# Retention chunks and a Mish layer on one core: outer products as half-array matmuls behind the present terms, states kept as 64x64 blocks, and two products in exchanged order

## The chip, the core and the metric

The kernel runs on one core of one Trainium2 chip. The metric is device time in microseconds (us), the median of some runs. The kernel before took 203.49 us (three runs, 203.35 to 203.62). The engines are TensorE (PE: matmuls, and PEld for its weight loads), VectorE (DVE), ScalarE (ACT), GpSimd (POOL) and SyncE (SP, which here only issues DMAs).

## The reference

Two stages. The first is a linear recurrence for 4 batches and 8 heads over 768 steps with head size 64, the second a two-layer net on its output.

```
gamma = 1.0 - 2.0 ** (-5.0 - np.arange(H))
for t in range(S):
    state = gamma * state + k[t] (outer) v[t]        # 64 x 64 per batch and head
    y[t] = scale * (q[t] @ state)
x = y as (B * S, H * D)                              # 3072 x 512
h = x @ w_in                                         # 512 x 2048
g = h * tanh(log(1 + exp(h)))                        # Mish
return g @ w_out                                     # 2048 x 512
```

## The kernel before

**Chunks.** The recurrence is done in chunks of 128 steps; a batch has 6 of them (`NCH`), so there are 24 chunks, numbered g through all batches. For a chunk the kernel makes the scores k·q (`scores`, L387), masks them to the lower triangle on DVE (`mask`, L397), and adds two terms into one PSUM tile `y_ps`: the past term, state times q (`past`, L430), and the present term, masked scores times v (`present`, L437). The decay factors are folded into the casts of q and v to 16 bits, which POOL makes (`cast_q`, L328, and `cast_v`, L343); k comes through POOL's DMA queue as 16 bits (`bring_k`, L333); the transposed q and k come by DMA on SP's queue (`turn_by_dma`, L356).

**States.** The state after chunk g is (u + state before) times gamma^128, where u is the outer product k·v over the 128 steps of the chunk (`outer`, L404). Two heads share one 128x128 matmul: the four pairs of heads give a tile of 128 x 512, in which the two diagonal 64x64 blocks of each pair are the wanted states, and the other two blocks are mixed products of two different heads. The factor tile `gcm` holds gamma^128 in the diagonal blocks and zero elsewhere, so that the multiplication also clears the mixed blocks. `state_sum` (L412) adds u and the state before on DVE, `state_decay` (L421) multiplies by `gcm`, on POOL in the later blocks. At the first chunk of a batch there is no state before, and `state_sum` multiplies at once (L416). The last chunk of a batch needs no state. `past` uses the 128x128 tile of a pair of heads as weights.

**Blocks.** The second stage takes the chunks in blocks: block 0 has 4 chunks, blocks 1 to 10 have 2 each (256 rows). Block 0 and the weights fill the first 51.5 us. In block 1 only the first layer is done by the seven-product method, in blocks 2 to 10 both layers are:

- `g1_seven` (L617) makes h for half of its tiles with seven products of quarter size instead of eight (`mm`, L636: eight matmuls of 128x128 weights by 128 columns each, L639), from sums and differences of weights (`wsum`) and of x (`tsums`, made by `x_sums`, L608), and the other half with four plain products (`plain`, L659: eight matmuls by 256 columns, L663). Three PSUM tiles pb, px and pe are used again within a block: ACT copies an intermediate value out (`snap`, L643), and the next product then adds onto the tile in place. DVE adds a copy to a tile (`plus`, L654) for c11, c22 and c12, and ACT applies Mish to g.
- `seven` (L714) does the same for the second layer (`mm`, L733, 256 columns), with sums of g (`gsum`) that DVE makes, and ACT's copies `snap` (L738) m1, u2, m5.

The order of everything is written by hand: the pool of schedules is off (`manual_schedule`), so each engine carries out its instructions in the order of the Python text. `steps_of(blk)` (L953) names what is put between the products of a block: after the second product ("p2"), behind some later ones ("p6", "p7", "p4", "h2", "end"), and in `seven` ("m2", "m7", "m3"). While block `blk` is computed, `nb = blk + 1` gets ready: its first chunk is a - 2 and its second a - 1, where a = first[blk] + 4. In "p2" stand the outer products of both chunks of nb (`outer_next`, L933), the sum and the decay of the first; in "p7" the sum of the second, in "m2" its decay; in "h2" the scores of both; in "m7" the past and present terms (`y_two`, L479), whose result ACT copies to 16 bits (L489); in "m3" the sums of x for the next block. Block 1 has a plan of its own (`plan_of`, L985).

The order of the products in `g1_seven`, with what each of them waits for: a(0,0) into px, which ACT copies as m1; a(0,1) into pb (c11 = pb + m1); "p2"; then s(2) added into px (copy u2) and s(1) into pe (copy m5), in this order where nb has two outer products (`sum_first`), else in the other; plain(1,0); s(3) added into px, for which u2 must have been read; c22 = px + m5 on DVE; s(4) added into pe, for which m5 must have been read; c12 = pe + u2; "p7"; plain(3,0); a(1,1) added into px, for which c22 must have been read; plain(1,1); scores ("h2"); plain(3,1).

Two PSUM rings hold all this: `mmps` with 4 tiles for the second stage, `atps` with 2 for scores, u and y.

Of the kernel before, what the change touches and what calls it, by code (L numbers as in the profile page):

```python
# [9 lines left out]
FP16 = mybir.dt.float16  # L10
FP32 = mybir.dt.float32
AF = mybir.ActivationFunctionType
ALU = mybir.AluOpType
# [3 lines left out]
def kernel(  # L17
# [21 lines left out]
    BLOCKS = [4] + [2] * ((NCK - 4) // 2)  # L39
    first = [sum(BLOCKS[:i]) for i in range(len(BLOCKS))]  # L40
# [3 lines left out]
    FPS = NFB // NSL  # L44
# [36 lines left out]
    ident = cpool.tile([P, P], FP16, name="ident")  # L81
    tri = cpool.tile([P, C], FP32, name="tri")
    gcm = cpool.tile([P, HP, P], FP32, name="gcm")
    warm = cpool.tile([P, 1], FP32, name="warm")
    gate_t = cpool.tile([P, 1], FP16, name="gate")
    nc.gpsimd.memset(ident, 0.0)
# [18 lines left out]
    for h in range(H):  # L105
        o = 64 * (h % 2)
        nc.vector.memset(gcm[o:o + 64, h // 2, o:o + 64], float(gamma[h] ** C))

    win_ap = moe_w_in.rearrange("(bp p) f -> p bp f", p=P)
# [3 lines left out]
    raw, k16s, v16s, t16s, kts, amf = {}, {}, {}, {}, {}, {}  # L113
    loaded, cast, qkts, ats, ams, states, us, ys, sus = {}, {}, {}, {}, {}, {}, {}, {}, {}
    xts, gts, wins, wouts, wtmps = {}, {}, {}, {}, {}
    gtiles, tmats, gsums = {}, [], []
# [8 lines left out]

    def room(g):
        loaded[g] = [
            lpool.tile([P, H, D], FP32, name=nm + "f", tag=nm + "f", bufs=4 if nm == "q" else 6)
            if g < BRING or nm != "k" else None for nm in "qkv"]

    def load_one(g, n, queue):
# [89 lines left out]
            eng.tensor_copy(dst, src)  # L221

    def load_two(nm, s, half):
        t = lpool.tile([P, HP, R, D], FP32, name=nm + "f", tag=nm + "f", bufs=6)
# [179 lines left out]
    def outer(g, u_ps):  # L404
        _, k16, v16, _ = cast[g]
        for i in range(HP):
            nc.tensor.matmul(  # L407
                u_ps[:, i], k16[:, 2 * i:2 * i + 2], v16[:, 2 * i:2 * i + 2],
                start=True, stop=True)
        us[g] = u_ps  # L410

    def state_sum(g):  # L412
        u_ps = us.pop(g)
        if g % NCH == 0:
            states[g] = stp.tile([P, HP, P], FP16, name="st")
            nc.vector.tensor_tensor(states[g], u_ps, gcm, op=ALU.mult)  # L416
        else:
            sus[g] = stp.tile([P, HP, P], FP32, name="su")
            nc.vector.tensor_tensor(sus[g], u_ps, states[g - 1], op=ALU.add)  # L419

    def state_decay(g, by):  # L421
        if g in sus:
            states[g] = stp.tile([P, HP, P], FP16, name="st")
            by.tensor_tensor(states[g], sus.pop(g), gcm, op=ALU.mult)  # L424

    def state(g):
        state_sum(g)
        state_decay(g, nc.vector)

    def past(g, y, fresh, pairs=range(HP)):  # L430
        st, qt = states[g - 1], qkts[g][0]
# [15 lines left out]
    def last_of_batch(g):  # L447
        return g % NCH == NCH - 1
# [3 lines left out]
    def scores_one(g):  # L452
        scores(g)
        mask(g)

    def outer_state(g):
        outer(g, atps.tile([P, 2, HP, P], FP32, name="u_ps", tag="at")[:, 0])
        state(g)

    def scores_two(blk):
        a = first[blk]
# [3 lines left out]
        mask(a + 1)  # L467

    def outer_two(blk):
        a = first[blk]  # L470
        u_ps = atps.tile([P, 2, HP, P], FP32, name="u_ps", tag="at")
        for j in range(2):
            if not last_of_batch(a + j):
                outer(a + j, u_ps[:, j])
        for j in range(2):
            if not last_of_batch(a + j):
                state(a + j)

    def y_two(blk):  # L479
        a = first[blk]  # L480
# [136 lines left out]
    def g1_seven(blk, steps, sum_first=False):  # L617
# [9 lines left out]
        def s(i):  # L627
            return lambda f, d: wsums[0][:, i - 1, d, f * P:(f + 1) * P]

        def b(i, j):  # L630
            return lambda d: x_part(blk, i, j)[:, d]

        def t(i):
            return lambda d: tsums[blk][:, i - 1, d]

        def mm(h_ps, w, x, first=False):  # L636
            for f in range(FPS):
                for d in range(n):
                    nc.tensor.matmul(  # L639
                        h_ps[:, f], w(f, d), x(d), start=first and f == 0 and d == 0,  # L640
                        stop=d == n - 1, skip_group_check=True)
# [33 lines left out]
        mm(pb, a(0, 1), b(1, 0), True)  # L675
        c11 = plus(pb, m1)
        step("p2")
        if sum_first:
            mm(px, s(2), t(2))
            u2 = snap(px)  # L680
        mm(pe, s(1), t(1), True)
        m5 = snap(pe)
        if not sum_first:
            mm(px, s(2), t(2))
            u2 = snap(px)
        step("u2")
        mish_of(0, 0, c11)
        step("p6")
        plain(1, 0)
        mm(px, s(3), t(3))  # L690
        c22 = plus(px, m5)
        mm(pe, s(4), b(1, 1))
        c12 = plus(pe, u2)
        mish_of(1, 1, c22)
        mish_of(0, 1, c12)
# [115 lines left out]
    def first_block():  # L811
# [9 lines left out]
        at = at_tile()  # L821
# [62 lines left out]
        for s in range(1, NSL):  # L884
# [12 lines left out]
            24: [(turn, CPB)],  # L897
            25: [(scores_one, CPB)],
            27: [(turn, CPB + 1)],
            28: [(outer_state, CPB), (casts, CPB + 2), (turn_and_load, CPB + 2), (cast_q, CPB + 3)],  # L900
            29: [(scores_one, CPB + 1)],
            31: [(y_two, 1)],
        }
# [26 lines left out]
            turn_by_dma(g)  # L930
            load_to(g + 3)

    def outer_next(blk):  # L933
        a = first[blk]
        u_ps = atps.tile([P, 2, HP, P], FP32, name="u_ps", tag="at")
        for j in range(2):
            if not last_of_batch(a + j):
                outer(a + j, u_ps[:, j])

    def sum_next(blk, j):  # L940
        if not last_of_batch(first[blk] + j):
            state_sum(first[blk] + j)

    def decay_next(blk, j):
        state_decay(first[blk] + j, nc.gpsimd)

    def gate_x(blk):
        gate(tsums[blk][:, 3, 0, :1])
# [24 lines left out]

# [22 lines left out]
    for blk in range(1, len(BLOCKS)):  # L996
        if blk >= SEVEN:
            steps = steps_of(blk)
            g1_seven(blk, steps, blk + 1 < len(BLOCKS) and not last_of_batch(first[blk + 1] + 1))
# [49 lines left out]
```

## Time and profile before

| | |
|---|---|
| median of three runs | 203.49 us |
| the profiled execution | 204.0 us, its span 202.2 us |
| granted TensorE clock in the profile | 0.999 |
| start-up with block 0 | 0 to 51.5 us, PE busy 46.3 |
| block 1 | 51.5 to 67.3 us, PE busy 15.7 |
| blocks 2 to 9 | 67.3 to 186.1 us, PE busy as good as all of it, 14.7 to 15.0 us a block |
| block 10 and the end | 186.1 to 202.2 us, PE busy 12.9 |
| in a block of 14.7 us | DVE busy 11.0, ACT 8.1, POOL 7.8 |

The span is the time from the first to the last instruction; the execution's own time has 1.8 us around it. A row of the groups reads: line, engine, operation, output and inputs, shape, count, busy time in all, mean ns of one, then the idle time of its engine ahead of it and what ended it. A row of the timeline reads: start, length, engine, line, operation, count, and in brackets the idle time before. A matmul's length there includes its way through the array, so that matmuls overlap; what one costs PE is the distance from start to start.

### The profile page before, as it was taken

The page shows a single profiled execution, that of the slowest core. Times are in us where ns is not written, and L with a number is a line of the kernel's source. Part 1 is how long each engine was busy: PE and PEld are TensorE (multiplying, and loading weights), DVE is VectorE, ACT ScalarE, POOL GpSimd, SP SyncE. Part 2 cuts the span into 40 slices and gives each one's busy share as a digit, 9 for nine tenths or more (in the row PEclk, how much of TensorE's full clock was granted, in tenths as well). Part 3 has the DMA queues.
Part 4 walks back from the last instruction along what each step waited for, and adds up shares of the span by engine and source line. Part 5 has one row for each costly group of instructions (what it writes and reads, how often), then busy time and mean ns, then how long its engine had stood idle before and what let it go on. Part 6 is the DMA issues. An engine that isn't in the chain of part 4 may idle for free.

```text
span 202.2 us, 5401 instructions
## 1 busy us (share of the span) xinstructions
PE 193.7 (96%) x2239; PEld 153.0 (76%) x2239; DVE 143.9 (71%) x271; ACT 102.6 (51%) x183; POOL 82.4 (41%) x99
## 2 busy tenths in 40 slices
PE   6897999989999999999999999999999999999993
PEld 2455544445865888988988988988988988989982
DVE  2777693969848687588696696787696696596552
ACT  2363664151960572673573573563663753753840
POOL 4072000617645347646608629626609716200000
PEclk9999999999999999999999999999999999999999
DMA  5999999999899999999991998999992992200202
GB/s 163 303 312 357 386 386 305 270 255 194 150 116 273 253 201 202 144 176 211 188 183 49 151 165 174 167 172 156 209 200 62 186 136 56 105 3 28 80 26 78
DMA packets 95896, 36.55 MB, mean 181 GB/s; under 512 B 82304, under 2 KB 89984, under 8 KB 95872
## 3 DMA queue, kind: packets, MB, share of 16 engines
q1 hardware_dynamic: 75968, 33.30, 73.1%
q0 software_dynamic: 16640, 2.10, 16.4%
q10 hardware_dynamic: 3264, 0.82, 2.3%
q8 instruction: 17, 0.28, 0.6%
q14 instruction: 7, 0.06, 0.1%
HBM read 27.30 MB, written 6.29 MB: 166 GB/s over the span
## 4 chain that ended last, share of the span: by engine, by line
PE 80%; DMA 8%; DVE 6%; ACT 2%; issue 1%; SPq 0%; DVEq 0%
PE o_ps L734 28%; PE h_ps L663 18%; PE h_ps L639 16%; DMA wt<-in_moe_w_out_dram 6%; PE o_ps L526 6%; PE y_ps L443 3%; PE at L393 3%; DMA qfirst<-in_q_dram 2%; PE y_ps L433 2%; PE u_ps L407 2%; DVE tmat L558 1%; PE h_ps L807 1%; ACT xt L489 1%; DVE tmat L560 1%; DVE tmat L559 1%
## 5 line engine op out<-in xcount | busy, mean ns | idle before, releaser
L663 PE MATMUL h_ps<-xt,win 128*128 128x256 f16 x320 | 41.2, 273 | 0.0
L330 POOL TENSOR_TENSOR qk<-qf,qvs 128x512 f16<-128x512 f32 x20 | 24.0, 1199 | 25.5 <-DMA qf<-in_q_dram 25.3
L663 PEld LDWEIGHTS <-win 128*128 128x128 f16 x320 | 29.4, 98 | 3.6
L734 PEld LDWEIGHTS <-gsum 128*128 128x128 f16 x288 | 27.5, 98 | 3.8
L656 DVE TENSOR_TENSOR hsum<-h_ps,hsnap 128x512 f32<-128x512 f32 x30 | 19.8, 688 | 13.7 <-PE h_ps L639 11.4
L399 DVE TENSOR_TENSOR am<-at,tri 128x1024 f16<-128x1024 f32 x20 | 24.2, 1217 | 3.6 <-PE at L393 3.6
L667 ACT ACTIVATE g<-h_ps 128x512 f16<-128x512 f32 x40 | 23.8, 594 | 5.6 <-PE h_ps L663 5.5
L646 ACT COPY hsnap<-h_ps 128x512 f32<-128x512 f32 x30 | 16.6, 588 | 17.6 <-PE h_ps L639 17.6
L734 PE MATMUL o_ps<-tmat,gsum 128*128 128x256 f16 x216 | 25.1, 273 | 0.0
L345 POOL TENSOR_TENSOR v<-vf,qvs 128x512 f16<-128x512 f32 x20 | 21.3, 1063 | 5.2 <-DMA vf<-in_v_dram 5.2
L734 PEld LDWEIGHTS <-g 128*128 128x128 f16 x216 | 21.1, 98 | 2.4
L748 DVE TENSOR_TENSOR osb<-o_ps,snap 128x256 f32<-128x256 f32 x27 | 11.4, 424 | 16.0 <-PE o_ps L734 11.3
L526 PE MATMUL o_ps<-wout,g 128*128 128x512 f16 x96 | 22.7, 379 | 0.0
L489 ACT CAST xt<-y_ps 128x1024 f16<-128x1024 f32 x10 | 10.1, 1012 | 21.9 <-PE y_ps L443 21.9
L650 ACT ACTIVATE g<-hsum 128x512 f16<-128x512 f32 x30 | 18.7, 634 | 4.0 <-DVE hsum L656 4.0
L740 ACT COPY snap<-o_ps 128x256 f32<-128x256 f32 x27 | 10.1, 373 | 19.4 <-PE o_ps L734 19.4
L639 PEld LDWEIGHTS <-wsum 128*128 128x128 f16 x320 | 19.1, 98 | 0.5
L734 PE MATMUL o_ps<-wout,g 128*128 128x256 f16 x144 | 17.2, 273 | 0.0
L354 POOL COPY gate<-gsum 128x1 f16<-128x1 f16 x8 | 1.5, 183 | 37.9 <-DVE gsum L708 37.9
L639 PE MATMUL h_ps<-xsum,wsum 128*128 128x128 f16 x240 | 16.6, 219 | 0.0
L424 POOL TENSOR_TENSOR st<-su,gcm 128x512 f16<-128x512 f32 x11 | 13.9, 1267 | 6.1 <-DVE su L419 6.1
L639 PEld LDWEIGHTS <-win 128*128 128x128 f16 x240 | 15.1, 98 | 1.5 <-issue 0.8
(97 smaller groups left out, 294.0 us busy)
## 6 DMA issues: line engine op xcount, KB each, us to landing
vf<-in_v_dram SPq DMA_DIRECT2D x23, 256.0 KB, 5.7
out_dram<-osb SPq DMA_DIRECT2D x22, 256.0 KB, 4.9
qf<-in_q_dram SPq DMA_DIRECT2D x19, 256.0 KB, 5.5
wt<-in_moe_w_out_dram SPq DMA_DIRECT2D x3, 1024.0 KB, 9.2
wi<-in_moe_w_in_dram SPq DMA_DIRECT2D x4, 512.0 KB, 7.4
wi<-in_moe_w_in_dram SPq DMA_DIRECT2D x2, 1024.0 KB, 11.7
qk<-in_k_dram POOLq DMA_DIRECT2D x16, 128.0 KB, 5.4
kf<-in_k_dram SPq DMA_DIRECT2D x7, 256.0 KB, 6.0
```

The lines of the kernel that those rows point to most:

```text
L330: nc.gpsimd.tensor_tensor(room16(g)[0], loaded[g][0], qs.unsqueeze(2).broadcast_to((P, H, D)), op=ALU.mult)
L345: nc.gpsimd.tensor_tensor(room16(g)[2], loaded[g][2], vs.unsqueeze(2).broadcast_to((P, H, D)), op=ALU.mult)
L399: nc.vector.tensor_tensor(am, ats.pop(g), tri.unsqueeze(1).unsqueeze(1).broadcast_to((P, 2, HP, C)), op=ALU.mult)
L424: by.tensor_tensor(states[g], sus.pop(g), gcm, op=ALU.mult)
L526: nc.tensor.matmul(o_ps, gts[blk, fb][:, t * P:(t + 1) * P], wouts[s][:, f, cols], start=(fb == 0), stop=(fb == NFB - 1))
L639: nc.tensor.matmul(h_ps[:, f], w(f, d), x(d), start=first and f == 0 and d == 0, stop=d == n - 1, skip_group_check=True)
L646: nc.scalar.copy(x, h_ps)
L650: nc.scalar.activation(gt[:, 2 * i * FPS:(2 * i + 1) * FPS, j * P:(j + 1) * P], h, AF.Mish, scale=inv_boost3)
L656: nc.vector.tensor_tensor(h, h_ps, x, op=ALU.add)
L663: nc.tensor.matmul(h_ps[:, j], win(s, 2 * half + j, bp), xt(blk, bp), start=bp == 0, stop=bp == NBP - 1)
L667: nc.scalar.activation(gt[:, fb:fb + 2], h_ps, AF.Mish, scale=inv_boost3)
L734: nc.tensor.matmul(o_ps, x(f), w(f), start=first and f == 0, stop=f == n - 1, skip_group_check=True)
```

## The change

- `outer` makes eight matmuls for a chunk instead of four: each head alone, 128x64 weights by 64 columns, the two heads of a pair to the upper and the lower 64 partitions of PSUM. The tile u has 4 x 64 columns, without mixed blocks. Only chunk 4, at the end of block 0, keeps the old form (`outer_wide`).
- The sum and the decay work on 128 x 256 elements (`suc`, `stc`), the factors `gcv` are one per partition and pair.
- `spread_state`: ACT copies the two 64-partition halves of `stc` into the diagonal blocks of one of three tiles `stx` that POOL has zeroed at the start; `past` reads these.
- The outer products of the second chunk of block nb and the first chunk of the block behind it (`handed_on`) now stand in "m7" of block blk, behind `y_two(nb)`, whose present terms are half-array matmuls too. In "p2" and "p7" stand the sums of chunks whose outer product was made one block earlier; the spread of chunk a - 3 stands in "p7", that of a - 2 in "m7" ahead of `y_two`. In block 1 the outer product of chunk 6 stands alone at step 12, those of 7 and 8 behind `y_two(2)`.
- `g1_seven` has one order now: s(1) into pe, s(2) into px, and behind plain(1,0) s(4) into pe ahead of s(3) into px. c22 is still added before c12.
- The rings of the loaded k have 4 tiles instead of 6.

```diff
     def outer(g, u_ps):
         _, k16, v16, _ = cast[g]
         for i in range(HP):
-            nc.tensor.matmul(
-                u_ps[:, i], k16[:, 2 * i:2 * i + 2], v16[:, 2 * i:2 * i + 2],
-                start=True, stop=True)
+            for hh in range(2):
+                nc.tensor.matmul(
+                    u_ps[64 * hh:64 * hh + 64, i], k16[:, 2 * i + hh], v16[:, 2 * i + hh],
+                    start=i == 0, stop=True, skip_group_check=True)
         us[g] = u_ps
 
     def state_sum(g):
         u_ps = us.pop(g)
         if g % NCH == 0:
-            states[g] = stp.tile([P, HP, P], FP16, name="st")
-            nc.vector.tensor_tensor(states[g], u_ps, gcm, op=ALU.mult)
+            stcs[g] = stp.tile([P, HP, D], FP16, name="stc", tag="stc")
+            nc.vector.tensor_tensor(stcs[g], u_ps, decay, op=ALU.mult)
         else:
-            sus[g] = stp.tile([P, HP, P], FP32, name="su")
-            nc.vector.tensor_tensor(sus[g], u_ps, states[g - 1], op=ALU.add)
+            sus[g] = stp.tile([P, HP, D], FP32, name="suc", tag="suc")
+            nc.vector.tensor_tensor(sus[g], u_ps, stcs[g - 1], op=ALU.add)
...
+    def spread_state(g):
+        states[g] = stx[g % 3]
+        for hh in range(2):
+            o = slice(64 * hh, 64 * hh + 64)
+            nc.scalar.copy(states[g][o, :, o], stcs[g][o])
...
+    def handed_on(blk):
+        return [g for g in (first[blk] + 1, first[blk] + 2) if g < NCK and not last_of_batch(g)]
...
     def outer_two(blk):
-        a = first[blk]
-        u_ps = atps.tile([P, 2, HP, P], FP32, name="u_ps", tag="at")
-        for j in range(2):
-            if not last_of_batch(a + j):
-                outer(a + j, u_ps[:, j])
-        for j in range(2):
-            if not last_of_batch(a + j):
-                state(a + j)
+        gs = handed_on(blk)
+        if gs:
+            u_ps = u_tile()
+        for j, g in enumerate(gs):
+            outer(g, u_ps[:, j, :, :D])
...
         step("p2")
-        if sum_first:
-            mm(px, s(2), t(2))
-            u2 = snap(px)
         mm(pe, s(1), t(1), True)
         m5 = snap(pe)
-        if not sum_first:
-            mm(px, s(2), t(2))
-            u2 = snap(px)
+        mm(px, s(2), t(2))
+        u2 = snap(px)
         step("u2")
         mish_of(0, 0, c11)
         step("p6")
         plain(1, 0)
+        mm(pe, s(4), b(1, 1))
         mm(px, s(3), t(3))
         c22 = plus(px, m5)
-        mm(pe, s(4), b(1, 1))
         c12 = plus(pe, u2)
...
-            "p2": [*then((gate_x, blk), (cast_q, a)), *only((outer_next, nb), (sum_next, nb, 0),
-                   (decay_next, nb, 0)), (cast_v, a), (bring_k, a + 1)],
+            "p2": [*then((gate_x, blk), (cast_q, a)), (sum_next, a - 3), (decay_next, a - 3),
+                   (cast_v, a), (bring_k, a + 1)],
...
-            "p7": [(store_due, 2), *only((sum_next, nb, 1)), (sums_a, blk, slice(0, FPS))],
+            "p7": [(store_due, 2), (sum_next, a - 2), (spread_next, a - 3), (sums_a, blk, slice(0, FPS))],
...
-            "m2": [*only((gate_g, blk), (decay_next, nb, 1)), (cast_q, a + 1), (cast_v, a + 1),
+            "m2": [*only((gate_g, blk), (decay_next, a - 2)), (cast_q, a + 1), (cast_v, a + 1),
...
-            "m7": only((y_two, nb)),
+            "m7": only((spread_next, a - 2), (y_two, nb), (outer_two, nb)),
...
-                12: [(outer_two, blk + 1), (cast_v, a + 1), (bring_k, a + 2),
+                12: [(outer_state, first[blk] + 2), (cast_v, a + 1), (bring_k, a + 2),
                      (turn_and_load, a + 1)],
-                14: [(y_two, blk + 1)]}
+                14: [(y_two, blk + 1), (outer_two, blk + 1)]}
```

More of the change, by code (lines that the diff above doesn't have):

```diff
@@ L83 @@
     gcm = cpool.tile([P, HP, P], FP32, name="gcm")
+    gcv = cpool.tile([P, HP], FP32, name="gcv")
+    stx = [cpool.tile([P, HP, P], FP16, name=f"stx{i}") for i in range(3)]
     warm = cpool.tile([P, 1], FP32, name="warm")
@@ L107 @@
         nc.vector.memset(gcm[o:o + 64, h // 2, o:o + 64], float(gamma[h] ** C))
+        nc.vector.memset(gcv[o:o + 64, h // 2:h // 2 + 1], float(gamma[h] ** C))
+    decay = gcv.unsqueeze(2).broadcast_to((P, HP, D))
+    for t in stx:
+        nc.gpsimd.memset(t, 0.0)
     win_ap = moe_w_in.rearrange("(bp p) f -> p bp f", p=P)
@@ L113 @@
     raw, k16s, v16s, t16s, kts, amf = {}, {}, {}, {}, {}, {}
+    stcs = {}
     loaded, cast, qkts, ats, ams, states, us, ys, sus = {}, {}, {}, {}, {}, {}, {}, {}, {}
@@ L127, in room @@
         loaded[g] = [
-            lpool.tile([P, H, D], FP32, name=nm + "f", tag=nm + "f", bufs=4 if nm == "q" else 6)
+            lpool.tile([P, H, D], FP32, name=nm + "f", tag=nm + "f", bufs=6 if nm == "v" else 4)
             if g < BRING or nm != "k" else None for nm in "qkv"]
@@ L223, in load_two @@
     def load_two(nm, s, half):
-        t = lpool.tile([P, HP, R, D], FP32, name=nm + "f", tag=nm + "f", bufs=6)
+        t = lpool.tile([P, HP, R, D], FP32, name=nm + "f", tag=nm + "f", bufs=6 if nm == "v" else 4)
         nc.sync.dma_start(
@@ L414, in state_sum @@
         if g % NCH == 0:
-            states[g] = stp.tile([P, HP, P], FP16, name="st")
-            nc.vector.tensor_tensor(states[g], u_ps, gcm, op=ALU.mult)
-        else:
-            sus[g] = stp.tile([P, HP, P], FP32, name="su")
-            nc.vector.tensor_tensor(sus[g], u_ps, states[g - 1], op=ALU.add)
+            stcs[g] = stp.tile([P, HP, D], FP16, name="stc", tag="stc")
+            nc.vector.tensor_tensor(stcs[g], u_ps, decay, op=ALU.mult)
+        else:
+            sus[g] = stp.tile([P, HP, D], FP32, name="suc", tag="suc")
+            nc.vector.tensor_tensor(sus[g], u_ps, stcs[g - 1], op=ALU.add)
     def state_decay(g, by):
         if g in sus:
-            states[g] = stp.tile([P, HP, P], FP16, name="st")
-            by.tensor_tensor(states[g], sus.pop(g), gcm, op=ALU.mult)
+            stcs[g] = stp.tile([P, HP, D], FP16, name="stc", tag="stc")
+            by.tensor_tensor(stcs[g], sus.pop(g), decay, op=ALU.mult)
+    def spread_state(g):
[3 more added lines that the diff above has]
+            nc.scalar.copy(states[g][o, :, o], stcs[g][o])
     def state(g):
@@ L428, in state, with outer_wide @@
         state_decay(g, nc.vector)
+        spread_state(g)
+    def outer_wide(g):
+        _, k16, v16, _ = cast[g]
+        u_ps = u_tile()[:, 0]
+        for i in range(HP):
+            nc.tensor.matmul(
+                u_ps[:, i], k16[:, 2 * i:2 * i + 2], v16[:, 2 * i:2 * i + 2],
+                start=True, stop=True)
+        su = stp.tile([P, HP, P], FP32, name="su", bufs=1)
+        nc.vector.tensor_tensor(su, u_ps, states[g - 1], op=ALU.add)
+        states[g] = stp.tile([P, HP, P], FP16, name="st")
+        nc.vector.tensor_tensor(states[g], su, gcm, op=ALU.mult)
     def past(g, y, fresh, pairs=range(HP)):
@@ L454, in scores_one, with u_tile @@
         mask(g)
+    def u_tile():
+        return atps.tile([P, 2, HP, P], FP32, name="u_ps", tag="at")
     def outer_state(g):
-        outer(g, atps.tile([P, 2, HP, P], FP32, name="u_ps", tag="at")[:, 0])
+        outer(g, u_tile()[:, 0, :, :D])
         state(g)
+    def handed_on(blk):
+        return [g for g in (first[blk] + 1, first[blk] + 2) if g < NCK and not last_of_batch(g)]
     def scores_two(blk):
@@ L615, in x_sums, with g1_seven @@
         nc.vector.tensor_tensor(t[:, 3], b[1][0], t[:, 1], op=sub)
-    def g1_seven(blk, steps, sum_first=False):
+    def g1_seven(blk, steps):
         n = NBP // 2
@@ L899, in first_block @@
             27: [(turn, CPB + 1)],
-            28: [(outer_state, CPB), (casts, CPB + 2), (turn_and_load, CPB + 2), (cast_q, CPB + 3)],
+            28: [(outer_wide, CPB), (casts, CPB + 2), (turn_and_load, CPB + 2), (cast_q, CPB + 3)],
             29: [(scores_one, CPB + 1)],
@@ L931, in turn_and_load, with sum_next, decay_next, spread_next @@
             load_to(g + 3)
[L933 to L945, printed above, removed]
+    def sum_next(g):
+        if g in us:
+            state_sum(g)
+    def decay_next(g):
+        state_decay(g, nc.gpsimd)
+    def spread_next(g):
+        if g in stcs:
+            spread_state(g)
     def gate_x(blk):
@@ L998 @@
             steps = steps_of(blk)
-            g1_seven(blk, steps, blk + 1 < len(BLOCKS) and not last_of_batch(first[blk + 1] + 1))
+            g1_seven(blk, steps)
             seven(blk, steps, blk + 1 == len(BLOCKS))
```

## The prediction

> **What bounds the kernel now.** I read the page's busy shares first, then the chain of work that ended last, then the timeline of one block after the start-up, record by record.
>
> ```profile
> PE 193.7 (96%) x2239; PEld 153.0 (76%) x2239; DVE 143.9 (71%) x271; ACT 102.6 (51%) x183; POOL 82.4 (41%) x99
> ...
> PE 80%; DMA 8%; DVE 6%; ACT 2%; issue 1%; SPq 0%; DVEq 0%
> ```
>
> TensorE (PE) is busy 96%, and the chain is PE for 80%; its DMA and DVE parts lie before 51.5 us. From 51.5 us to the last product PE goes from one product to the next: blocks of 14.7 to 15.0 us. So an edit is worth what it adds to or takes from PE's row of instructions, plus any wait that it puts in front of one. The 71% of VectorE (DVE), 51% of ScalarE (ACT) and 41% of GpSimd (POOL) count only where PE waits for them.
>
> **The outer products.** Single records of the block at 82.3 us give the cadences: a full 128x128 matmul with 128 moving columns starts every 56 ns (L433, L407), one with 256 every 109 ns. Half-array matmuls go in pairs:
>
> ```profile
> 94.23 0.61 PE L433 MATMUL y_ps<-qkt,st 128*128 128x128 f16 x8
> 94.77 0.64 PE L443 MATMUL y_ps<-am,v 128*64 128x128 f16 x16
> 95.34 0.28 PE L734 MATMUL o_ps<-wout,gsum 128*128 128x256 f16 x1
> ```
>
> The 16 half matmuls of L443 are 8 pairs, 56 ns apart, 2 to 4 ns within a pair. Going into this form costs 93 ns more than a usual step (94.617 to 94.766) and 24 ns in the first pair; coming out 95 ns (95.185 to 95.336) and 11. That is 0.22 us for a visit. The 15 narrow outer products follow L443 in the same form, so 14 of them pay no visit; the one of chunk 6, in the block at 51.5 us, stands alone and pays it.
>
> Removed: 15 outers of four matmuls, 15 x 0.223 = 3.35 us. Added: 15 x 4 pairs of 64 moving columns. No row has such a pair. From below: half the moving columns, half of 56, 28 ns; PE can issue that fast, for L268 starts four weight loads and four matmuls per 56 ns. From above: 30 + 24 = 54 ns, if the 24 ns that the first matmul of L443 waits for its weights (243 ns against 219) is not hidden. In the later pairs of L443 it is hidden, so I take 30 ns, near the lower end: 0.12 us an outer, 1.80 in all. Sum **-3.35 + 1.80 + 0.22 = -1.33 us**; the ends give -1.45 and +0.11.
>
> The Trainium skill speaks against this gain (TensorEngine Tiling (Array Packing), Restrictions; TensorE: Matmul & The Clock Gate, LDWEIGHTS): column tiling turns fast weight load off, and a load then takes columns / 1.2 ns, 53 ns for 64. By that a pair takes 53 ns, and the gain is gone. The 24 ns of the trace do not agree with 53.
>
> **The two swapped products.** Call T the first matmul of a block and count in starts: a small product (L639, eight matmuls) takes 0.447 us, a plain one (L663) 0.873. The last block (T = 186.07) has no outers and so has today's order as the new one will have it:
>
> ```profile
> 186.97 1.06 PE L639 MATMUL h_ps<-xsum,wsum 128*128 128x128 f16 x16
> 187.86 1.04 PE L663 MATMUL h_ps<-xt,win 128*128 128x256 f16 x8
> 188.79 0.61 PE L639 MATMUL h_ps<-xsum,wsum 128*128 128x128 f16 x8
> 189.24 0.61 PE L639 MATMUL h_ps<-xt,wsum 128*128 128x128 f16 x8
> 189.68 1.04 PE L663 MATMUL h_ps<-xt,win 128*128 128x256 f16 x8
> 190.56 0.61 PE L639 MATMUL h_ps<-xsum,win 128*128 128x128 f16 x8
> ...
> 189.51 1.29 DVE L656 TENSOR_TENSOR hsum<-h_ps,hsnap 128x512 f32<-128x512 f32 x2 [1.47 <-PE h_ps L639]
> ```
>
> The product at 188.79 is `mm(px, s(3), t(3))`: it waited 0.06 us for ACT's copy `u2` (ended 188.742). Four blocks of the seven kind have that wait. At 189.51 DVE adds `c22` from px, 0.327 us after px's last matmul started, for 0.692 us, to 190.20; the next product that accumulates into px, at 190.56, has to wait for that read and has 0.31 us to spare, which is `mm(pe, s(4))` standing between. The swap puts pe first. Then px is ready for u2 by far (T + 3.11 against T + 2.67), but between px's first matmul and the next use of px there are only 0.447 + 0.873 = 1.320 us, and the read takes 0.387 + 0.327 + 0.692 + 0.045 (DVE to PE, as at 15.41 to 15.45) = 1.451. That is 0.131 us of PE wait in each of ten blocks. **+1.31 - 4 x 0.06 = +1.07 us.** Every term has a row; DVE has been idle 1.47 us before `c22`, so nothing else moves it. The ends: 0.08 to 0.18 a block, +0.6 to +1.6.
>
> **The states.** DVE's sum falls from 683 ns (L419) to about 424 (L748, 128x256 from PSUM), POOL's decay from 1267 to about 640. Neither shortens anything: in the list of waits PE waits for a sum once, 0.4 us in the start-up at an outer that stays as it is, and for a decay never. What is added is ACT's spreading: two copies per chunk of 64 partitions x 256. One pair stands behind the mish of c12 and ahead of three mishes. Followed through the block (c22 mish T + 4.55, c12 T + 5.15, copies T + 5.68, then three at 0.48 us spacing) the mish of plain(1,1) ends at T + 7.83, and PE's weight load for it comes at T + 7.96: hidden, by 0.08 us after the way to PE. ACT's 0.69 us idle ahead of its last mish is that cover.
>
> The other pair is not hidden. In ACT's queue it comes behind the copy `m5` of seven(), and PE's next instructions are `past`, which reads the spread state:
>
> ```profile
> 93.55 0.37 ACT L740 COPY snap<-o_ps 128x256 f32<-128x256 f32 x1 [0.45 <-PE o_ps L734]
> 95.44 1.01 ACT L489 CAST xt<-y_ps 128x1024 f16<-128x1024 f32 x1 [1.52 <-PE y_ps L443]
> ...
> L740 ACT COPY snap<-o_ps 128x256 f32<-128x256 f32 x27 | 10.1, 373 | 19.4 <-PE o_ps L734 19.4
> ...
> L341 ACT CAST qk<-kf 128x512 f16<-128x512 f32 x4 | 2.5, 622 | 8.4 <-DMA qf<-in_q_dram 4.8 <-DMA kf<-in_k_dram 3.6
> ```
>
> ACT copies follow each other 0.10 us before the end of the one before (L646: 588 ns, spacing 482). L740 gives 373 ns for 256 elements from PSUM; from SBUF 512 elements take 34 ns more than from PSUM (622 against 588), so I estimate a copy at 0.407. From the start of m5: copies at +0.27 and +0.57, end +0.975, at PE +1.04 (0.051 us from an ACT end to PE, 188.742 to 188.793, and 0.015 for the weight load). PE wants the state at +0.897 where `past` of the even chunk comes first (94.450 - 93.553), and at +0.673 where a batch starts (109.187 - 108.514). That is 0.143 us in six blocks and 0.367 in two. In the block at 51.5 us the chain is: outer 6, DVE's mult after the copy that ends at 64.21, two copies, about 0.2 us after `past` would start. **0.86 + 0.73 + 0.20 = +1.79 us.** Ends: 0 if a copy costs the 202 ns of ACT's smallest instruction (L103); 3.7 if copies of 407 ns do not overlap at all.
>
> **At nothing:** the memsets (eight on DVE at a 0.163 us step, done by 4.1 us, where it waits for q until 5.48; three on POOL, some 1.5 us, done by 4.5, where it waits for v until 9.78); the k ring of 4 instead of 6 (its first four tiles are cast by 14.0 us, the next loads start at 31.4); SP's queue, which keeps its order. POOL's decays wait for nothing new and are shorter, so cast_v and bring_k behind them come no later; the outers' k and v of a later chunk are ready, for bring_k lands 5.4 us after an issue one block earlier.
>
> **Sum.** -1.33 + 1.07 + 1.79 = +1.53 us. The profiled execution took 204.0 us with a span of 202.2, the median shown is 203.49; I put the sum on both: 205.5 and 203.7 for a profile, **205.0 us** for the median, 0.8% slower.
>
> **Rivals.**
> 1. Not slower: the spread arrives in time. Place: the wait of `past` for ACT. It turns on the copies: if the second ends by +0.83 (below about 0.26 us each, spaced 0.2 or less), PE waits only at batch starts or never, and the sum is -1.33 + 1.07 = -0.26: 203.2 us. If the wait at px is shorter than the row says by as much, down to 202.2. For it: 64 partitions, 16-bit source, idle ACT. Against: L740, and L255's 16-bit source is no faster (587 ns).
> 2. Half-array pairs at 54 ns, the weights not hidden: outers +0.11, total +2.97, 206.5 us. Against: the later pairs of L443.
> 3. The first pair of copies takes the 0.08 us left ahead of plain(1,1)'s mish, if copies do not overlap: 0.2 - 0.08 = 0.12 us there in six blocks, and 3.7 - 1.8 = 1.9 more at `past`: 207.6 us. No row shows two such copies in a row.
> 4. The swap pays: PE does not wait at px, and the waits for u2 go: -1.33 - 0.24 + 1.79, 203.7 us. Against: the 0.692 us of `c22` lie in every block.
>
> Chances: forecast 0.52 (204.2 to 205.9), rival 1 0.23 (0.14 of it faster by over 0.2%), rival 2 0.12, rival 3 0.07, rival 4 0.06. A measurement of this kernel can tell about 0.2% (0.4 us) from no change. Faster 0.15, same 0.14 (the rest of rival 1, and rival 4), slower 0.71. The range leaves out some 0.1 on each side: 202.8 to 206.8 us.
>
> **What the profile after would show.** Outers: the starts of 64-column pairs, 28 to 30 ns apart (54 is rival 2), and no gap between L443's last and the first outer. Swap: before the product into px after plain(3,0), a gap of 0.13 us, ended by DVE's `c22`; none ahead of s(3). Spread: in `past`, a wait for ACT's spread, 0.14 us in most blocks and 0.37 at batch starts. Wrong would be: blocks under 14.7 us with two outers, `past` at a 56 ns cadence right after its neighbours, or PE waiting for POOL or a transfer that I cost at nothing.

## The result and the profile after

The changed kernel takes **207.0 us** (median of four runs, 206.46 to 207.24), the kernel before 203.42 (203.06 to 203.62) beside it: a ratio of 1.0174, 95% interval 1.0149 to 1.0199. It is slower by 3.6 us, where +1.53 was forecast and 206.8 was the end of the range. The profiled execution took 207.24 us with a span of 205.5 (before 204.0 and 202.2), at a granted clock of 1.0.

The page of the changed kernel, busy shares and the chain that ended last:

```profile
PE 195.4 (95%) x2299; PEld 150.9 (73%) x2299; DVE 138.7 (68%) x278; ACT 114.6 (56%) x213; POOL 77.2 (38%) x103
...
PE 74%; DMA 8%; DVE 8%; ACT 7%; issue 2%; SPq 0%; DVEq 0%; ACTq 0%
```

PE's share of the chain fell from 80% to 74%, ACT's rose from 2% to 7%: what set the end for longer is ScalarE. The chain at one block boundary says where (pieces in order of time: start, us, what):

```profile
90.83 2.93 PE o_ps L758 x26
93.76 0.02 issue
93.78 0.37 ACT snap L764
94.16 0.03 issue
94.18 0.41 ACT stx L438
94.59 0.01 issue
94.60 0.41 ACT stx L438
95.01 0.05 issue
95.06 0.40 PE y_ps L460 x4
95.45 0.57 PE y_ps L470 x16
96.02 0.12 PE u_ps L415 x8
```

Read the "issue" pieces. The copy m5 (L764) ends at 94.156, the first spreading copy starts 0.025 us *behind* that end, the second 0.012 behind the end of the first, and `past` (L460) goes on at 95.055, where PE had wanted the state at 94.68. The prediction had let each of these copies start 0.10 ahead of the end of the one before, as two neighbouring copies of L646 do in the kernel before. One row of its timeline and one of the changed kernel's show the difference (start, length of the two together):

```profile
99.14 1.07 ACT L646 COPY hsnap<-h_ps 128x512 f32<-128x512 f32 x2 [0.81 <-PE h_ps L639]
...
94.18 0.82 ACT L438 COPY stx<-stc 64x256 f16<-64x256 f16 x2
```

Two copies of 588 ns take 1.07 us, 0.10 less than their sum; two of about 400 ns take 0.82, 0.01 more than theirs. The list of waits sums it up (us in total, times, longest):

```profile
PEld L460 <- ACT stx L438: 4.1, 9, 0.6
...
PE y_ps L460 <- ACT stx L438: 2.0, 9, 0.3
```

The weight load's 4.1 us and the matmul's 2.0 lie partly over each other. Taken from the single records, as what the start of a matmul lies behind its usual step, the stops of PE from 40 us on sum to 10.78 us against 5.78 before (visits to the half-array form included). Of the 5.0 us more:

| where PE stops | predicted | in the trace after |
|---|---|---|
| `past`, for the spread | 6 x 0.143 + 2 x 0.367 + 0.20 = 1.79 | 6 x 0.373 + 2 x 0.466 + 0.314 = 3.48 |
| the product into px, for c22 | 10 x 0.131 = 1.31 | 10 x 0.142 = 1.42 |
| s(3), for u2 (4 x 0.06 before) | -0.24 | -0.24 |
| weights from plain(1,1)'s mish | 0 | 6 x 0.066 = 0.40 |

These sum to 5.06. The outers give back -15 x 0.223 + 15 x 4 x 0.030 + 0.2 = -1.3, so that +3.8 is explained; the last product starts 3.2 us later in the profile, and the time is 3.6 us longer. (In these two profiles the last weight transfer lands at 44.13 us before and at 43.47 after, in those of the other runs between 43.4 and 44.0; sums over the span do not close better than that.)

The rows of the new operations, from the groups kept apart by shape (busy us, mean ns of one, then idle time before them):

```profile
L438 ACT COPY stx<-stc 64x256 f16<-64x256 f16 x30 | 12.0, 400 | 5.9 <-DVE stc L424 5.5
L432 POOL TENSOR_TENSOR stc<-suc,gcv 128x256 f16<-128x256 f32 x12 | 7.3, 609 | 6.2 <-DVE suc L427 6.2
...
L427 DVE TENSOR_TENSOR suc<-u_ps,stc 128x256 f32<-128x256 f32 x12 | 5.0, 413 | 0.0
...
L415 PE MATMUL u_ps<-v,qk 128*64 128x64 f16 x120 | 3.4, 196 | 0.0
```

The duration of a copy, 400 ns, is what was estimated (407); so are the sum of 413 and the decay of 609 (424, 640). Only the *spacing* of the copies was not.

### The profile page after: what moved, and what is told of

It reads as the page before. It is cut to its first block, busy times and chain, and to the rows that moved or that the text cites. A ratio compares the mean times of both kernels' runs of the same rounds, so it can differ in the third digit from the quotient of the medians.

```text
span 205.5 us, 5562 instructions
## 1 busy us (share of the span) xinstructions
PE 195.4 (95%) x2299; PEld 150.9 (73%) x2299; DVE 138.7 (68%) x278; ACT 114.6 (56%) x213; POOL 77.2 (38%) x103
## 4 chain that ended last, share of the span: by engine, by line
PE 74%; DMA 8%; DVE 8%; ACT 7%; issue 2%; SPq 0%; DVEq 0%; ACTq 0%
PE o_ps L758 24%; PE h_ps L691 17%; PE h_ps L667 16%; DMA wt<-in_moe_w_out_dram 6%; PE o_ps L554 4%; ACT stx L438 3%; PE y_ps L470 3%; PE at L400 3%; DMA qfirst<-in_q_dram 2%; PE y_ps L460 2%; ACT snap L764 1%; DVE am L406 1%; PE h_ps L831 1%; DVE tmat L586 1%; PE u_ps L415 1%
## 5 line engine op out<-in xcount | busy, mean ns | idle before, releaser
L337 POOL TENSOR_TENSOR qk<-qf,qvs 128x512 f16<-128x512 f32 x20 | 21.8, 1089 | 23.6 <-DMA qf<-in_q_dram 23.5
L352 POOL TENSOR_TENSOR v<-vf,qvs 128x512 f16<-128x512 f32 x20 | 23.5, 1174 | 5.6 <-DMA vf<-in_v_dram 5.6
L695 ACT ACTIVATE g<-h_ps 128x512 f16<-128x512 f32 x40 | 22.8, 596 | 0.9 <-PE h_ps L691 0.8
L758 PEld LDWEIGHTS <-g 128*128 128x128 f16 x216 | 20.6, 98 | 3.4 <-ACT g L695 1.1
L764 ACT COPY snap<-o_ps 128x256 f32<-128x256 f32 x27 | 10.1, 373 | 17.5 <-PE o_ps L758 17.2
L758 PE MATMUL o_ps<-wout,g 128*128 128x256 f16 x144 | 17.7, 273 | 0.0
L554 PEld LDWEIGHTS <-g 128*128 128x128 f16 x96 | 8.8, 98 | 9.7 <-issue 0.3
```

What stands on the lines that cost most here:

```text
L337: nc.gpsimd.tensor_tensor(room16(g)[0], loaded[g][0], qs.unsqueeze(2).broadcast_to((P, H, D)), op=ALU.mult)
L352: nc.gpsimd.tensor_tensor(room16(g)[2], loaded[g][2], vs.unsqueeze(2).broadcast_to((P, H, D)), op=ALU.mult)
L554: nc.tensor.matmul(o_ps, gts[blk, fb][:, t * P:(t + 1) * P], wouts[s][:, f, cols], start=(fb == 0), stop=(fb == NFB - 1))
L695: nc.scalar.activation(gt[:, fb:fb + 2], h_ps, AF.Mish, scale=inv_boost3)
L758: nc.tensor.matmul(o_ps, x(f), w(f), start=first and f == 0, stop=f == n - 1, skip_group_check=True)
L764: nc.scalar.copy(x, o_ps)
```

## The experiments

**Theory A**: the terms are those of the prediction and they add up; two of them were too small, because ScalarE's spreading copies run strictly one after another. **Rival B**: the late state is not the cause, but ScalarE's whole load of 30 more copies (114.6 us busy against 102.6), which would stay whatever past reads. **Rival C**: the swapped products cost nothing, or even gain. Each run below stands beside runs of the kernel before on the same chip (medians 203.38 in the first four runs, 203.49 in the others).

**The old order of the two products, everything else as changed.**

```diff
-        mm(pe, s(4), b(1, 1))
         mm(px, s(3), t(3))
         c22 = plus(px, m5)
+        mm(pe, s(4), b(1, 1))
         c12 = plus(pe, u2)
```

> The changed kernel (207.0 us) with the two small products put back in the old order: s(3) into px ahead of s(4) into pe. Theory A, the terms add: the wait at px (0.142 us in ten blocks, read in its trace) goes, ACT's copy u2 is waited for about 0.06 us in each block instead, and the 0.066 us that six blocks wait for the mish of plain(1,1) goes, since c22 is 0.45 us earlier: -1.4 + 0.6 - 0.4 = -1.2, 205.8 us. Theory B, that the rise comes from ACT's 12 us of new copies or from the place of the outer products and the swap only moves a wait: 207.0 us, within 0.3.

Measured: 206.06 us, ratio 1.0136 [1.0110, 1.0162], 0.94 less than the changed kernel. The ten waits of 0.142 are gone, nine of 0.06 for u2 are there, the six of 0.066 in front of plain(1,1)'s weights are gone as well, and the waits of `past` are what they were (0.374 in six blocks, 0.467 in two). Net by the records: -1.42 + 0.54 - 0.40 = -1.28. The interval of this ratio and that of the changed kernel overlap a little, so the records carry this reading more than the 0.94.

**The swap alone, in the kernel before.**

```diff
+        mm(pe, s(4), b(1, 1))
         mm(px, s(3), t(3))
         c22 = plus(px, m5)
-        mm(pe, s(4), b(1, 1))
```

> The kernel before (203.4 us) with the swap alone: s(4) into pe ahead of s(3) into px. Theory A: 0.14 us of wait for c22 ahead of a(1,1) in ten blocks, less the four waits of 0.06 us for u2: +1.2 us, 204.6 us. Theory C, that the swap is harmless and the wait in the changed kernel comes with the other edits: 203.2 us (the four waits gone).

Measured: 205.17 us, ratio 1.0087 [1.0065, 1.0109], +1.79, some 0.6 above A's number. C falls: in a kernel with no spreading at all the swap costs by itself. Its timeline, at one block (start, length, engine, line, tiles; the DVE row holds c22 and then c12):

```profile
85.30 0.61 PE L639 MATMUL h_ps<-xsum,wsum 128*128 128x128 f16 x8
85.74 1.04 PE L663 MATMUL h_ps<-xt,win 128*128 128x256 f16 x8
86.02 1.29 DVE L656 TENSOR_TENSOR hsum<-h_ps,hsnap 128x512 f32<-128x512 f32 x2 [1.44 <-PE h_ps L639]
...
86.76 0.61 PE L639 MATMUL h_ps<-xsum,win 128*128 128x128 f16 x8
```

From the product of L663 to the next are 1.02 us where its eight matmuls take 0.873: 0.14 us in which the product that accumulates into px waits for DVE's read of px, 86.02 to 86.71. By the records this wait is 10 x 0.142 = 1.42 us; in the five blocks in which s(1) comes second, s(4) now waits 0.06 for the copy of pe as well, and the four waits of s(3) for u2 (0.24) are gone: 1.72 against 0.24, so +1.5 of the +1.79.

**The late pair of copies left out.** `past` then reads the tiles with an older state: 16 of the 30 copies are left out and the terms of the past are another state's.

```diff
+    def no_spread(g):
+        states[g] = stx[g % 3]
...
-            "m7": only((spread_next, a - 2), (y_two, nb), (outer_two, nb)),
+            "m7": only((no_spread, a - 2), (y_two, nb), (outer_two, nb)),
```

> The changed kernel without the second spread of a block (that of chunk a - 2, in front of the past terms): the past term reads what lies in the tile, an older state, and 16 of the 30 copies are left out. Theory A: PE's wait in the past terms goes, 6 x 0.373 + 2 x 0.466 = 3.2 us: 203.8 us. Theory B (ACT's load as a whole, spread over the block): half of the copies, at most half of the rise of 3.6 us: 205.2 us or more.

Measured: 204.12 us, ratio 1.0033 [1.0018, 1.0048]. The waits of `past` are gone but for the 0.314 in block 1, whose copies stay; those for c22 (0.142) and in front of plain(1,1) (0.066) remain: 2.9 us of the 3.6 hang on these copies. The time is below B's 205.2, but the copies themselves went too; the next run keeps them.

**All copies kept, but the present terms and the outers put ahead of `past`**, so that PE has 0.7 us of work between its last product and the state.

```diff
-        if inter:
-            past(a, lambda i: y_ps[:, i, 0], lambda i: i % 2 == 0)
-        past(a + 1, lambda i: y_ps[:, i, 1], lambda i: not inter and i % 2 == 0)
         for j in range(2):
-            present(a + j, lambda i: y_ps[:, i, j], lambda i: False)
+            present(a + j, lambda i: y_ps[:, i, j], lambda i: j == 0 and i % 2 == 0)
+        if blk > 1:
+            outer_two(blk)
+        if inter:
+            past(a, lambda i: y_ps[:, i, 0], lambda i: False)
+        past(a + 1, lambda i: y_ps[:, i, 1], lambda i: False)
...
-            "m7": only((spread_next, a - 2), (y_two, nb), (outer_two, nb)),
+            "m7": only((spread_next, a - 2), (y_two, nb)),
...
-                14: [(y_two, blk + 1), (outer_two, blk + 1)]}
+                14: [(y_two, blk + 1)]}
```

> The changed kernel with all copies and all products, in another order behind s(3) of the second layer: present terms first, then the outer products, then the past terms, which alone read the spread state. ACT is as busy as before. Theory A: the present terms (0.45 us) and the outers (0.12 to 0.25) cover the 0.37 to 0.47 us, so that the wait goes and nothing else changes: 3.2 us less, 203.8 us. Theory B (ACT's load): 207.0 us.

Measured: 204.48 us, ratio 1.0036 [1.0010, 1.0062]. ScalarE is as busy as in the changed kernel (114.5 us), and 2.5 us are gone with the waits of `past`. It is 0.7 above A's number: at the starts of blocks 1 and 2 the profile has stops of 0.4 us, where the changed kernel's has none at the first and 0.05 and 0.20 near the second, and the kernel before 0.3 at both. B falls.

**The late copies put ahead of m5 in ScalarE's queue.** ScalarE is idle for 0.45 us there, and the decayed state is ready 0.16 us after that time begins (93.34 and 93.50 in the block whose chain is shown above).

```diff
         mm(pe, s(1), t(1), True)
+        step("m5")
         m5 = snap(pe)
...
+            "m5": only((spread_next, a - 2)),
-            "m7": only((spread_next, a - 2), (y_two, nb), (outer_two, nb)),
+            "m7": only((y_two, nb), (outer_two, nb)),
```

> The changed kernel (207.0 us) with the second pair of spreading copies put ahead of the copy m5 in ScalarE's queue, nothing else moved. Theory A (ScalarE runs its copies one after another, so that two of 0.40 us behind m5 end 0.37 us too late in six blocks and 0.47 in two): both copies fit between the end of GpSimd's decay and the moment at which past wants them, m5 comes some 0.6 us later and nobody wants it before VectorE's add, so the 3.17 us of waits go and 203.8 us is left. Rival D (what past waits for is ScalarE's whole load, and the wait only changes its place): the delayed m5 is what PE or VectorE waits for next, and the time stays above 205.5.

Measured: 204.11 us, ratio 1.0025 [1.0007, 1.0043]. In its timeline m5 now follows the copies and nobody waits:

```profile
93.31 0.82 ACT L438 COPY stx<-stc 64x256 f16<-64x256 f16 x2 [0.19 <-POOL stc L432]
94.13 0.54 PEld L460 LDWEIGHTS <-stx 128*128 128x128 f16 x8
94.15 0.37 ACT L764 COPY snap<-o_ps 128x256 f32<-128x256 f32 x1
94.24 0.61 PE L460 MATMUL y_ps<-qkt,stx 128*128 128x128 f16 x8
```

The eight matmuls of `past` take 0.61 us from the first start to the last end, without the stop in the middle. Only the 0.314 in block 1 is left. D falls: 2.9 us went by moving two copies ahead of one other. They start 0.93 us ahead of the first matmul of `past`, where it was 0.28.

**The same, and the old order of the products.**

> As the run before, and the two swapped products back in their old order. Theory A: the terms add, so another 0.9 to 1.2 us go (ten waits of 0.142 and six of 0.066, less about nine of 0.06 for u2 that come back): 202.8 us, that is 0.3% faster than the kernel before; what is left of the change is the outers' gain less the wait in the first of the blocks with sevens. Rival D: not below 204.

Measured: **202.83 us**, ratio 0.9967 [0.9950, 0.9984]: faster than the kernel before, by the interval 0.2 to 0.5%. From its page:

```profile
PE 192.8 (96%) x2299; PEld 151.6 (75%) x2299; DVE 140.2 (70%) x278; ACT 114.8 (57%) x213; POOL 77.0 (38%) x103
...
PE 78%; DMA 8%; DVE 8%; ACT 2%; issue 2%; SPq 0%; DVEq 0%; ACTq 0%
```

ACT has its 2% of the chain again, with the same 115 us of work as in the changed kernel. What is left is, by the records, the outers' gain of 1.3 us, less 0.3 in block 1 and five more waits of 0.06 for u2: -0.7, where -0.66 was measured. No run has the outers' gain alone.

**No copies at all**: DVE's first product and POOL's decay write two halves of 64 partitions straight into the zeroed tiles, and the products are in the old order.

```diff
...
-            stcs[g] = stp.tile([P, HP, D], FP16, name="stc", tag="stc")
-            by.tensor_tensor(stcs[g], sus.pop(g), decay, op=ALU.mult)
+            states[g] = stx[g % 3]
+            su = sus.pop(g)
+            for hh in range(2):
+                o = slice(64 * hh, 64 * hh + 64)
+                by.tensor_tensor(states[g][o, :, o], su[o], decay[o], op=ALU.mult)
...
-            nc.scalar.copy(states[g][o, :, o], stcs[g][o])
...
```

> No copy on ScalarE at all: VectorE's first product and GpSimd's decay write their two halves of 64 partitions straight into the zeroed tiles, and VectorE's sum reads them there; products in the old order. Theory A: the waits for the spread go in all nine blocks, the wait in front of the mish of plain(1,1) too, and the swap's: 207.0 - 3.5 - 0.9 = 202.6 us, or somewhat less. Against it (rival E): an instruction on 64 partitions costs as much as one on 128 for the same length, so two halves on GpSimd take twice its 0.6 us; the decay then ends 0.6 us later, at the time at which past wants the state, and the block keeps a wait of 0.1 to 0.5 us: 203.5 to 206 us.

Measured: 203.06 us, ratio 0.9973 [0.9958, 0.9987], the same as the run before within their intervals. E's price is right and its consequence isn't:

```profile
L439 POOL TENSOR_TENSOR stx<-suc,gcv 64x256 f16<-64x256 f32 x24 | 14.6, 608 | 6.3 <-DVE suc L431 5.4
L431 DVE TENSOR_TENSOR suc<-u_ps,stx 64x256 f32<-64x256 f32 x24 | 10.0, 416 | 0.4
```

A half of 64 partitions takes POOL 608 ns where all 128 took 609, and DVE 416 where they took 413. But the second half still ends at 92.63 in the block where `past` starts at 93.45, and no wait of `past` is left, the one in block 1 included. Two stops elsewhere have grown to 0.33 us (one at the start of block 2, 0.20 in most of the other runs, one ahead of s(3) in one block, 0.06 in the others); DVE's sums of 0.86 us stand near both, which is no proof.

**Why don't the copies overlap?** In the kernel before, ScalarE's instructions had started 0.09 to 0.11 us ahead of the end of the one before, and the changed kernel still shows that nearly everywhere else. In what follows a spacing is the start of an instruction less the end of the one before it on ScalarE, so that a negative one is an overlap. First guess: the place of the tiles, since all of them have moved.

```diff
+    pad = cpool.tile([P, 120], FP32, name="pad")
+    nc.gpsimd.memset(pad, 0.0)
```

> The changed kernel with 480 bytes of unused room behind its constants, which puts the later tiles back to the addresses that they have in the kernel before; the constants and the zeroed tiles stay where they are. If the place of a tile decides whether a ScalarE instruction starts ahead of the end of the one before it (theory F), the mish of c11 starts 0.11 us ahead of that end again, as in the kernel before, where in the changed kernel it starts 0.024 behind it, and the copies into the zeroed tiles may change too. If the kinds of the two instructions decide (rival G), all these spacings stay: +0.024, and +0.012 between the two copies. The time stays within 0.5 us of 207.0 either way.

Measured: 207.76 us in one execution, and F falls: with the later tiles back at their addresses (by the sum of the tiles' sizes) every spacing stays as in the changed kernel (+0.012 between the two copies, +0.024 at the mish of c11). Then height and stride, each by itself:

```diff
-            nc.scalar.copy(states[g][o, :, o], stcs[g][o])
+            nc.scalar.copy(states[g][:, :, o], stcs[g])
```

> The changed kernel with both spreading copies made over all 128 partitions, each to the same columns as before, so that the tiles are no longer block diagonal (that part of the computation is changed). Theory H (the half height of 64 partitions keeps the next instruction from starting early): the second copy starts 0.10 us ahead of the end of the first instead of 0.012 behind it, the waits of past fall from 0.37 to about 0.26 us and that of plain(1,1)'s mish goes, some 206 us. Theory S (the strided destination, four groups of 64, keeps it) or theory N (neither): the spacing stays at +0.012 and the time at 207.

```diff
+    flat = [cpool.tile([P, HP, D], FP16, name=f"flat{i}") for i in range(2)]
...
-            nc.scalar.copy(states[g][o, :, o], stcs[g][o])
+            nc.scalar.copy(flat[g % 2][o], stcs[g][o])
```

> The changed kernel with both spreading copies written to an unstrided tile of their own, 64 partitions each as before; past reads the zeroed tiles, so that the terms of the older states are left out. Nobody waits for these copies, so the time falls to about 203.7 us, and only their spacing is asked. Theory S: the second starts 0.10 us ahead of the end of the first. Theories H and N: +0.012 as before. If the spacing stays in this run and in the one over all partitions, both height and stride are out as single causes.

Timeline rows of m5 and the two copies (x2), first over all 128 partitions, with PE's rows:

```profile
93.77 0.38 ACT L764 COPY snap<-o_ps 128x256 f32<-128x256 f32 x1 [0.45 <-PE o_ps L758]
94.04 0.71 ACT L438 COPY stx<-stc 128x256 f16<-128x256 f16 x2
94.34 0.32 PEld L460 LDWEIGHTS <-stx 128*128 128x128 f16 x4
94.45 0.76 PE L460 MATMUL y_ps<-qkt,stx 128*128 128x128 f16 x8
94.81 0.23 PEld L460 LDWEIGHTS <-stx 128*128 128x128 f16 x4 [0.15 <-ACT stx L438]
```

then 64 partitions into the unstrided tile:

```profile
93.48 0.37 ACT L765 COPY snap<-o_ps 128x256 f32<-128x256 f32 x1 [0.45 <-PE o_ps L759]
93.88 0.83 ACT L439 COPY flat<-stc 64x256 f16<-64x256 f16 x2
```

Two copies of about 0.40 us fill 0.71 us at full height and 0.83 at half height, and m5's end at 94.15 and 93.86 lies 0.10 behind the first copy's start in the one and 0.02 ahead of it in the other. **Theory H holds**: over 128 partitions all 15 pairs of copies start 0.09 to 0.105 us ahead of the first's end, so does every copy behind m5, and the mish of c11 is back at its -0.115. In the unstrided tile the second copy starts 0.024 behind the first's end in all pairs, those included in which it waits for no other engine, so S and N fall. Full height leaves waits at `past` of 0.143 in six blocks, 0.365 in two and 0.210 in block 1, 1.80 us, and none in front of plain(1,1)'s weights; one execution took 205.59 us (span 203.8). That is lower than H's own 206, since H had counted only the gain between the two copies and not the one behind m5. The unstrided run took 204.22 in one execution. One thing is not told apart: no run has two half-height copies in a row on the same 64 partitions, so the step from the lower to the upper half always comes with the half height.

## Why the prediction was wrong

**The direction, the place and the order of the steps were right; one premise was wrong and made two terms too small.** By its own steps:

- *The outers, -1.33*: right by the records. The pairs of L415 start at 95.853, 95.881, 95.913 and 95.944, 30 ns apart, with no gap behind L470. Rival 2 (54 ns) falls. The Trainium skill's two rules behind it (TensorEngine Tiling (Array Packing), Restrictions: column tiling turns fast weight load off; TensorE: Matmul & The Clock Gate, LDWEIGHTS: columns / 1.2 ns) would give, as an estimate, 53 ns for a load of 64 columns; at 30 ns a pair, two loads included, the trace doesn't show that price.
- *The swapped products, +1.07*: right. 0.142 us in each of ten blocks (predicted 0.131), the four waits of 0.06 gone: +1.18. Undoing it won 0.94, making it alone cost 1.79 where the waits are worth 1.5. Rival 4 falls.
- *The spread, +1.79*: **the step that failed** is its first premise, "ACT copies follow each other 0.10 us before the end of the one before", taken from L646's copies of 128 partitions from PSUM and set on copies of 64 partitions. The length was right (0.400 for 0.407), the decay was ready and the state was wanted when it said. But a copy of half height is not overlapped, and in six blocks not even the one behind m5, so it is 0.373, 0.466 and 0.314 instead of 0.143, 0.367 and 0.20: 3.48 us. The prediction had this case as the far end of the term, 3.7 for copies that do not overlap at all. The run at full height bears this out to the figure: with the overlap restored the trace shows 0.143, 0.365 and 0.210, and its one time of 205.59 stands beside the 205.5 that was given for a profile.
- *The first pair, hidden by 0.08 us*: wrong for the same reason. Without overlaps the copies take what was left, and PE waits 6 x 0.066 = 0.40 us for the weights of plain(1,1). It takes the new order of the products as well: with the old order this wait is gone. The prediction had worked this out as rival 3 (0.7 there and 1.9 at `past`, 207.6 us) and gave it 0.07, with the remark that no row showed two such copies in a row. That rival is what happened, at 0.40 and 1.69.
- *At nothing*: memsets, the shorter k ring, SP's queue and POOL's decays put no new stop on PE's row.

With 0.11 more for the swap, +1.53 + 1.69 + 0.40 + 0.11 = +3.7 us, where +3.6 was measured. So the error was in one borrowed row: a spacing, not a length, carried over to a shape that no row had. The chance of 0.07 was too low for a premise that carried 2.1 us and had no row of its own kind, and the range ended short of the bound that the text itself had named.

The Trainium skill's figure for the overlap (ScalarE: Activation LUTs, What ACT_TABLE_LOAD costs: back-to-back ACTIVATEs overlap by about 93 ns) agrees with the rows at 128 partitions in which nothing else is waited for, 0.09 to 0.13 us here, also for copies. At 64 partitions the measurement differs, +0.012 and +0.024, and decides.

**What stays open**: why the copy behind m5 does overlap in the two blocks where a batch starts (-0.104, its source then written by DVE) and the one behind c12's mish always (-0.094), and why in the changed kernel the mish of c11 starts +0.024 behind a full-height copy's end. With spreading copies of full height all of these start early, so the half-height copies are behind it. Two things narrow it down. The two blocks in which the copy behind m5 overlaps are also the two that have no first pair of copies, so DVE as the writer need not be the reason. And in the run without the late copies the mish of c11 is early (-0.115) in exactly the two blocks ahead of which the block before has no spreading copy at all, and at +0.024 in the other seven; in six of these eleven instructions of full height stand between the last spreading copy and the mish. So the effect reaches further than the next instruction, and why it shows at this one is not known. The time of the kernel does not hang on them, except for the 0.10 at m5, which is in the table above.

## What to carry to other kernels

A duration and a spacing are two measurements: before a row's overlap is used for a new instruction, look whether any row of that shape (partitions above all) stands behind another, and if none does, take the sum without overlap as the likely end, not as a far one. A small instruction on the path is moved before it is made faster: ScalarE had 0.45 us of idle time one copy earlier, and the same two copies put there cost `past` nothing in the eight blocks where they were moved. An exchange of two products is judged by the next use of the accumulator, since another engine's read of it stands between; here one product in between was 0.14 us too little, ten times.

## What the runs showed of the hardware

- Half the partitions don't save time: 400 ns at 64 partitions and 403 at 128 for ScalarE's copy of 256 elements, 416 and 413 for VectorE's sum, 608 and 609 for GpSimd's product. Work cut into two halves by partitions costs twice here.
- In these runs ScalarE starts nothing early behind an instruction on 64 partitions: 15 of 15 second copies at +0.011 or +0.012, the six mishes behind such a copy at +0.024, and m5 behind it at +0.024 in eight of eight where the copies were put ahead of it, against -0.09 to -0.115 at 128 in the kernel before. Two such copies hold it for 0.82 us instead of 0.71.
- Half-array matmuls in pairs with 64 moving columns start 30 ns a pair, and the visit costs the 0.09 us in and 0.10 us out that L443 showed, once for the present terms and the outers together.
